# Attention with beacon keys, then a maxout FFN: q and k turned on VectorE in 32x32 blocks, scores in four 32-row tiles

## The chip, the cores and the metric

The kernel runs on one core of a Trainium2 chip. The metric is device time in microseconds of one execution; the time before is the median of 3 runs, 336.58 us (336.32 to 336.59). A core has TensorE (PE; its weight loads are listed apart as PEld), VectorE (DVE), ScalarE (ACT), GpSimd (POOL) and SyncE (SP), each with its own instruction queue that it works through in order, and 16 DMA engines. SBUF is the working memory with 128 partitions; matrix products land in PSUM, which has 8 banks of 512 fp32 values per partition. All 8 banks are taken in both kernels.

## The reference

```python
# q, k, v: (8, 8, 576, 64) fp32; beacon_k, beacon_v: (8, 8, 16, 64)
k_all = np.concatenate([beacon_k, k], axis=2)          # 592 keys
v_all = np.concatenate([beacon_v, v], axis=2)
scores = scale * np.matmul(q, k_all.transpose(0, 1, 3, 2))
scores = np.where(causal, -1000000000.0, scores)       # beacons are never masked
scores = scores - scores.max(-1, keepdims=True)
a = np.exp(scores)
a /= a.sum(-1, keepdims=True) + 1e-09
attn = np.matmul(a, v_all)                             # (8, 8, 576, 64)
x = attn.transpose(0, 2, 1, 3).reshape(4608, 512)
h = np.maximum(np.maximum(x @ w1, x @ w2), x @ w3)     # (4608, 768)
out = h @ w_out                                        # (4608, 512) fp32
```

## The kernel before

All products are in bf16 with fp32 sums. For each batch of 576 tokens the eight heads are worked in four pairs ("p", 32 pairs in all), and two pairs make a quad of four heads (16 quads).

**Preparing q and k.** `load_pair` (L155) brings two heads of q and of k to 96 partitions with six tokens on each (token = 6*partition + r). `cast_pair` makes bf16 copies, mostly on POOL (L172). `turn` (L186) transposes them on PE, six 96x128 blocks for q, six for k and one small block for the beacons (L194, L200), into one PSUM bank each; `evac_q` and `evac_k` (L210, L217, L218) copy the result to SBUF on DVE. Queries stay in the order (r, partition), keys go back to token order. Each of the two heads of a pair gets its own 128-partition query tile `qz` whose other 64 partitions are zero, so that a product over 128 rows gives one head's scores.

**Scores.** A pair's 592 keys lie in five key tiles of 128 (the last has 80). `emit_scores` (L291) takes one of six chunks: per head one matmul (L306) into a PSUM bank of `sc_psum` (4 buffers) and one exponential on ACT (L314) into `at_sb`. The causal edge is put to zero on POOL, one `affine_select` per head (L332); in batch 0 a product with a mask on DVE does it (L329).

**Probabilities times values.** `pv_pass` (L344) works four heads at once in four 32-column tiles of the PE array: a pass with ones gives the sums (then Ln and Exp(-x) on ACT, L366 and L368), two passes with the even and odd columns of v give the outputs, which DVE multiplies by the reciprocals into `xT` (L373), a ring of four batches. `emit_pv` runs six such passes per quad, in three steps of two.

**FFN.** Blocks of 512 tokens; a block has 18 units of four matmuls (L396), each evacuated by ACT (the first of three, L404) or by a maximum on DVE (the other two, L406), and four units of six matmuls (L413) whose result DVE copies (L421) and SP stores (L429, two or three stores per tile because of the token order). Both kinds use `ffn_psum`, two buffers. 9 blocks make 198 units.

**Order.** Everything is emitted by hand in `emit_all` (L528): per chunk the scores, at some chunks a PV step of the quad before, the next pair's transposes, then the planned casts and loads (`at_step`, L499 on), filler matmuls in the first batch (`keep_busy`, L229), and FFN units as far as a running allowance and the finished batches let them. FFN units start with the second batch. The tail after the last PV step is FFN alone.

Of the kernel before, what the change touches and what calls it, by code (L numbers as in the profile page):

```python
# [16 lines left out]
def kernel(  # L17
# [27 lines left out]
    QR = 6  # L45
    QP = S // QR

    n_kt = (NK + 127) // 128
    k_rows = [min(128, NK - 128 * t) for t in range(n_kt)]

    k_tok = [128 * t - Nb for t in range(n_kt)]
    p_min = [max(0, t0) // QR for t0 in k_tok]
    p_max = [min(QP, -(-(k_tok[t] + k_rows[t]) // QR)) for t in range(n_kt)]
    q_wide = [QP - p0 for p0 in p_min]
    at_off = [QR * sum(q_wide[:t]) for t in range(n_kt + 1)]
    RH = QR // 2
    HALF = RH * QP
    n_quad = 2
    n_jj = H // (2 * n_quad)
    PPB = H // 2  # L60
    NPAIR = B * PPB

    RING = 4

    def head(g, j):
        return 4 * g + j

    def place(p):
        b, pi = divmod(p, PPB)
        return b, pi // n_jj, 2 * (pi % n_jj)  # L70
# [8 lines left out]
    st_pool = ctx.enter_context(tc.tile_pool(name="st", bufs=10))  # L79
    pair_pool = ctx.enter_context(tc.tile_pool(name="pair", bufs=3))  # L80
    bk_pool = ctx.enter_context(tc.tile_pool(name="bk", bufs=2))
    v_pool = ctx.enter_context(tc.tile_pool(name="v", bufs=2))
    kt_pool = ctx.enter_context(tc.tile_pool(name="kt", bufs=2))
# [4 lines left out]
    sc_psum = ctx.enter_context(tc.tile_pool(name="sc_psum", bufs=4, space=PSUM))  # L88
# [3 lines left out]

    busy = const.tile([128, 320], BF16, name="busy")
    nc.vector.memset(busy, 1.0)
    ident = const.tile([128, 128], BF16)
    make_identity(nc, ident)
    ones = const.tile([128, 32], BF16)
    nc.scalar.preload_act_table_set("natural_log_exp_and_others")


    NQZ = 2
    qz = []
    for i in range(NQZ):
        pair = []
        for e in range(2):
            z = const.tile([128, QR, QP], BF16, name=f"qz{i}{e}")
            nc.vector.memset(z[64 * (1 - e) : 64 * (1 - e) + 64], 0.0)
            pair.append(z)
        qz.append(pair)
    nc.vector.memset(ones, 1.0)  # L110


    MW = max(p_max[t] - p_min[t] for t in range(n_kt))
    mask = const.tile([128, n_kt, QR, MW], BF16, name="mask")
    nc.gpsimd.memset(mask, 1.0)
    for t in range(n_kt):
        nc.gpsimd.affine_select(
            out=mask[:, t],
            in_=mask[:, t],
            compare_op=ALU.is_ge,  # L120
            fill=0.0,
            base=QR * p_min[t] - k_tok[t],
            pattern=[[1, QR], [QR, MW]],
            channel_multiplier=-1,
        )


    STW = 4 * QR * D
    stage = {}

    def new_stage(key):
        stage[key] = st_pool.tile([128, STW], FP32, name="st")
        return stage[key]

    tiles = {}

    def v_tile(b):
        if b not in tiles:
            tiles[b] = v_pool.tile([128, n_kt, H, D], BF16, name="v_sb")
        return tiles[b]  # L140

    NQ2 = 2 * QR * D

    def load_beacon_k(b):
        st = bk_pool.tile([Nb, H, D], FP32, name="bk32")
        stage["bk", b] = st
        nc.sync.dma_start(out=st, in_=beacon_k[b].rearrange("h n d -> n h d"))

    def cast_beacon_k(b, cast):
        st = stage.pop(("bk", b))  # L150
        bk16 = bk_pool.tile([Nb, H, D], BF16, name="bk16")
        stage["bk16", b] = bk16
        cast(bk16, st)

    def load_pair(p, k_queue=None):  # L155
        b, g, j0 = place(p)
        hs = slice(head(g, j0), head(g, j0) + 2)
        st = new_stage(("pair", p))
        if g == 0 and j0 == 0:
            load_beacon_k(b)  # L160
        for i, (src, queue) in enumerate(((q, nc.sync), (k, k_queue or nc.sync))):
            queue.dma_start(
                out=st[0:QP, i * NQ2 : (i + 1) * NQ2].rearrange("p (h x) -> p h x", h=2),
                in_=src[b, hs].rearrange("h (p r) d -> p h (r d)", r=QR),
            )

    def cast_piece(p, i, cast, r0=0, r1=QR):

        st = stage["pair", p]
        if ("pair16", p, i) not in stage:  # L170
            stage["pair16", p, i] = pair_pool.tile([QP, QR, 2, D], BF16, name=f"p16{i}")
        cast(  # L172
            stage["pair16", p, i][:, r0:r1].rearrange("p r h d -> p h r d"),
            st[0:QP, i * NQ2 : (i + 1) * NQ2].rearrange(
                "p (h r d) -> p h r d", h=2, r=QR
            )[:, :, r0:r1],
        )

    def cast_pair(p, q_cast, k_cast):
        cast_piece(p, 0, q_cast)  # L180
        cast_piece(p, 1, k_cast)
        stage.pop(("pair", p))

    turned = {}

    def turn(p, i):  # L186
        b, g, j0 = place(p)
        src = stage.pop(("pair16", p, i))
        pool, name = (ffn_psum, "fps") if b == 0 else (sc_psum, "sc")
        ps = pool.tile([128, NK], BF16, name=name)  # L190
        if i == 1:
            bk16 = stage["bk16", b]
            h0 = head(g, j0)
            nc.tensor.transpose(  # L194
                ps[:, 0:Nb],
                bk16[:, h0 : h0 + 2].rearrange("p h d -> p (h d)"),
                ident[0:Nb, 0:Nb],
            )
        for r in range(QR):
            nc.tensor.transpose(  # L200
                ps[:, Nb + r * QP : Nb + (r + 1) * QP],
                src[:, r].rearrange("p h d -> p (h d)"),
                ident[0:QP, 0:QP],
            )
        return ps

    def evac_q(p, ps, copy=None):
        for e in range(2):
            hs = slice(64 * e, 64 * e + 64)
            (copy or nc.vector.tensor_copy)(  # L210
                qz[p % NQZ][e][hs], ps[hs, Nb:NK].rearrange("d (r p) -> d r p", r=QR)
            )

    def evac_k(p, ps):
        kT = kt_pool.tile([128, NK], BF16, name="kT")
        turned[p] = kT
        nc.vector.tensor_copy(kT[:, 0:Nb], ps[:, 0:Nb])  # L217
        nc.vector.tensor_copy(  # L218
            kT[:, Nb:NK].rearrange("d (p r) -> d p r", r=QR),
            ps[:, Nb:NK].rearrange("d (r p) -> d p r", r=QR),  # L220
        )

    def emit_transposes(p):
        q_ps = turn(p, 0)
        k_ps = turn(p, 1)
        evac_q(p, q_ps)
        evac_k(p, k_ps)

    def keep_busy(n, cols=320):  # L229
        ps = ffn_psum.tile([128, 512], FP32, name="fps")  # L230
        for _ in range(n):
            nc.tensor.matmul(
                ps[:, 0:cols], busy[:, 0:128], busy[:, 0:cols], start=True, stop=True
            )


    T_PIECES = [range(0, 3), range(3, n_kt)]

# [52 lines left out]
    def emit_scores(p, c, between=None):  # L291
# [28 lines left out]
        if between is not None:  # L320
            between()
# [281 lines left out]
```

## Time and profile before

| | before |
|---|---|
| median of 3 runs | 336.58 us |
| span of the profiled execution | 335.0 us (its own time outside the span is not listed apart; the median is 1.6 us more) |
| mean granted TensorE clock | 0.991 |
| PE busy | 317.1 us, 95% |
| DVE, ACT, POOL busy | 188.5, 186.7, 178.3 us |
| scores on PE (L306) | 384 matmuls, 77.5 us |
| exponentials (L314) | 384, 131.2 us |
| causal edge on POOL (L332) | 336, 93.5 us |
| moved by DMA | 42.02 MB, mean 125 GB/s |

The span runs from the first to the last instruction. Matmuls are pipelined: the time that one costs the PE is the distance to the next start, not the length of its own row, which holds its latency too. A row "x6" of the timeline merges six instructions that follow each other.

### The profile page before, as it was taken

What the parts mean: (1) busy time and instruction counts of PE and PEld (TensorE: products, weight loads), DVE (VectorE), ACT (ScalarE), POOL (GpSimd) and SP (SyncE); (2) the same over time, 40 slices, a digit from 0 to 9 for tenths busy, and PEclk for the clock granted to TensorE, in tenths of its full rate; (3) what the DMA queues carried; (4) which work ended last, traced back from release to release, by engine and by line L of the source; (5) the groups of instructions that cost most, each with busy time, mean ns of one, the idle gap of its engine ahead of it and who ended that gap; (6) DMA issues with size and microseconds to landing.
All of it is one profiled execution on the core that took longest, in us unless ns stands there. A gap on an engine that the chain in (4) does not pass through costs nothing.

```text
span 335.0 us, 9369 instructions
## 1 busy us (share of the span) xinstructions
PE 317.1 (95%) x3703; PEld 184.6 (55%) x3703; DVE 188.5 (56%) x368; ACT 186.7 (56%) x506; POOL 178.3 (53%) x469
## 2 busy tenths in 40 slices
PE   5886899996999999999999999999999999999994
PEld 2554556553555556555555878655555555544441
DVE  3675556662566556565666556555656465555553
ACT  3676667654766476747675667657664765220220
POOL 4778496646674686549564956485847733000000
PEclk9799999999999999999999999999999999999998
DMA  7999999998942681549162847130003001302204
GB/s 189 228 258 247 194 224 237 224 233 207 269 103 62 184 230 43 106 114 258 51 143 66 253 98 146 41 89 4 2 23 104 3 2 31 97 2 59 67 2 125
DMA packets 62971, 42.02 MB, mean 125 GB/s; under 512 B 42192, under 2 KB 58320, under 8 KB 62928
## 3 DMA queue, kind: packets, MB, share of 16 engines
q1 hardware_dynamic: 58672, 37.99, 47.7%
q0 software_dynamic: 4048, 3.15, 5.9%
q8 instruction: 29, 0.48, 0.6%
q10 hardware_dynamic: 208, 0.29, 0.3%
q14 instruction: 14, 0.11, 0.1%
HBM read 35.13 MB, written 9.44 MB: 133 GB/s over the span
## 4 chain that ended last, share of the span: by engine, by line
PE 86%; DVE 4%; ACT 4%; DMA 2%; SPq 1%; issue 1%; POOL 1%; DVEq 0%; ACTq 0%; POOLq 0%
PE fps L396 37%; PE sc L306 12%; PE fps L413 12%; PE pv L354 12%; PE sc L200 5%; PE sc L396 5%; ACT at_sb L314 3%; PE sc L413 2%; DVE at_sb L329 2%; DMA st<-in_q_dram 1%; PE sc L194 1%; DMA out_dram<-y 1%; DVE qz L210 1%; PE fps L200 1%; SPq L251 1%
## 5 line engine op out<-in xcount | busy, mean ns | idle before, releaser
L314 ACT ACTIVATE at_sb<-sc 128x288 bf16<-128x288 f32 (+4 forms) x384 | 131.2, 403 | 65.1 <-PE sc L306 57.5
L396 PE MATMUL fps<-xT,w_sb 128*128 128x512 bf16 (+1 forms) x648 | 147.1, 356 | 2.7 <-DVE y L421 2.2
L332 POOL TENSOR_SCALAR_AFFINE_SELECT at_sb<-at_sb 128x57 bf16<-128x57 bf16 (+1 forms) x336 | 93.5, 297 | 93.1 <-ACT at_sb L314 88.6
L396 PEld LDWEIGHTS <-w_sb 128*128 128x128 bf16 x720 | 66.8, 98 | 52.8 <-issue 3.2
L406 DVE TENSOR_TENSOR hT<-hT,fps 128x512 bf16<-128x512 bf16 x96 | 65.9, 686 | 52.2 <-PE fps L396 39.6
L306 PE MATMUL sc<-qz,kT 128*128 128x288 bf16 (+4 forms) x384 | 77.5, 286 | 5.9 <-ACT at_sb L314 3.9
L306 PEld LDWEIGHTS <-kT 128*128 128x128 bf16 (+1 forms) x384 | 38.0, 101 | 39.4 <-issue 5.2
L172 POOL CAST p<-st 96x768 bf16<-96x768 f32 x60 | 48.3, 829 | 7.6 <-DMA st<-in_k_dram 6.6
L404 ACT CAST hT<-fps 128x512 bf16<-128x512 f32 x48 | 28.1, 585 | 40.7 <-PE fps L396 40.4
L373 DVE TENSOR_TENSOR xT<-pv,recip 128x288 bf16<-128x288 f32 x64 | 27.7, 454 | 34.9 <-ACT recip L368 30.1
L413 PE MATMUL fps<-w_out_sb,hT 128*128 128x512 bf16 x192 | 46.8, 380 | 0.0
L421 DVE COPY y<-fps 128x512 f32<-128x512 f32 x32 | 22.1, 690 | 22.4 <-PE fps L413 12.2
L354 PE MATMUL pv<-at_sb,v_sb 128*32 128x288 bf16 (+4 forms) x1280 | 32.4, 237 | 0.0
L354 PEld LDWEIGHTS <-v_sb 128*32 128x32 bf16 (+1 forms) x1280 | 25.5, 96 | 11.8 <-issue 10.8
L413 PEld LDWEIGHTS <-hT 128*128 128x128 bf16 x216 | 19.5, 98 | 20.2 <-DVE hT L406 0.4
L210 DVE COPY qz<-sc 64x576 bf16<-64x576 bf16 x56 | 25.3, 451 | 8.1 <-PE sc L200 7.7
L200 PE MATMUL sc<-ident,p 96*128 96x96 bf16 x336 | 23.9, 207 | 0.1
L260 POOL CAST v_sb<-st 128x512 bf16<-128x512 f32 (+1 forms) x40 | 23.3, 614 | 0.6 <-DMA st<-in_v_dram 0.5
L200 PEld LDWEIGHTS <-p 96*128 96x128 bf16 x384 | 19.8, 98 | 6.4 <-DVE p L172 2.7
L218 DVE COPY kT<-sc 128x576 bf16<-128x576 bf16 x28 | 20.9, 748 | 0.0
L396 PE MATMUL sc<-xT,w_sb 128*128 128x512 bf16 x72 | 18.5, 379 | 0.0
L354 PE MATMUL pv<-at_sb,ones 80*32 80x42 bf16 (+4 forms) x640 | 17.9, 238 | 0.6 <-DVE xT L373 0.5
(36 smaller groups left out, 135.1 us busy)
## 6 DMA issues: line engine op xcount, KB each, us to landing
st<-in_q_dram SPq DMA_DIRECT2D x32, 288.0 KB, 5.1
st<-in_k_dram SPq DMA_DIRECT2D x31, 288.0 KB, 6.0
st<-in_v_dram SPq DMA_DIRECT2D x24, 256.0 KB, 4.6
out_dram<-y SPq DMA_DIRECT2D x24, 192.0 KB, 2.5
out_dram<-y SPq DMA_DIRECT2D x24, 128.0 KB, 2.4
w_sb<-in_moe_w_dram POOLq DMA_DIRECT2D x12, 192.0 KB, 9.1
st<-in_v_dram SPq DMA_DIRECT2D x8, 224.0 KB, 5.8
out_dram<-y SPq DMA_DIRECT2D x24, 64.0 KB, 2.0
```

The lines of the kernel that those rows point to most:

```text
L172: cast(stage["pair16", p, i][:, r0:r1].rearrange("p r h d -> p h r d"), st[0:QP, i * NQ2 : (i + 1) * NQ2].rearrange("p (h r d) -> p h r d" ...
L200: nc.tensor.transpose(ps[:, Nb + r * QP : Nb + (r + 1) * QP], src[:, r].rearrange("p h d -> p (h d)"), ident[0:QP, 0:QP],)
L210: (copy or nc.vector.tensor_copy)(qz[p % NQZ][e][hs], ps[hs, Nb:NK].rearrange("d (r p) -> d r p", r=QR))
L306: nc.tensor.matmul(ps[0:n, 0 : nr * w].rearrange("k (r p) -> k r p", p=w), kT[:, 128 * t : 128 * t + n], qz[p % NQZ][e][:, r0:r1, p0:QP], ...
L314: nc.scalar.activation(out=at_view(at_sb, t, j0 + e, r0, r1), in_=sc[e][0:n, 0 : nr * w], func=AF.Exp, scale=scale,)
L332: nc.gpsimd.affine_select(out=view[:, e], in_=view[:, e], compare_op=ALU.is_ge, fill=0.0, base=QR * p0 + r0 - k_tok[t], pattern=[[1, nr], ...
L354: nc.tensor.matmul(ps[32 * j : 32 * j + 32, :, p_min[t] : QP], lhsT, at_view(at_sb, t, j, hf * RH, (hf + 1) * RH).rearrange("k (r p) -> k ...
L373: nc.vector.tensor_mul(xs.rearrange("c (r p) -> c r p", p=QP), ps, recips[hf])
L396: nc.tensor.matmul(ps[:, o0 : o0 + n], w_in[i][:, ct, 128 * ft : 128 * (ft + 1)], xT[:, ct, x0 : x0 + n], start=(ct == 0), stop=(ct == n_c ...
L404: nc.scalar.copy(hT[:, ft, :], ps)
L406: nc.vector.tensor_max(hT[:, ft, :], hT[:, ft, :], ps)
L413: nc.tensor.matmul(ps, hT[:, ft, 128 * tt : 128 * (tt + 1)], w_out_sb[:, ft, :], start=(ft == 0), stop=(ft == n_ft - 1),)
```

## The change

q and k are loaded four heads at a time, 32 partitions per head and 18 tokens on each (token = 18*partition + s). After the cast to bf16 one DVE instruction transposes 36 blocks of 32x32, so that head h has its dimensions on partitions 32h to 32h+31, in two halves j of 32 dimensions side by side, and the tokens in order. A score block is then a sum over the two halves, of products over 32 rows, and the four heads go to four row tiles of the PE array and to four PSUM banks. Key tiles are put together in four bursts per quad. One exponential takes two banks, one `affine_select` four heads. The PE transposes, their evacuations, the zeroed query tiles, the mask tile and the filler matmuls are gone. Tokens are in order everywhere, so one store writes an output tile. A step is now a burst of a quad (16 x 4 steps): PV passes of the quad before, scores, planned work, FFN units.

```diff
-    QR = 6
-    QP = S // QR
+    HG = 4
+    n_quad = H // HG
+    NQ = B * n_quad
+    QS = S // 32
+    DJ = D // 32
+    q_min = [max(0, 128 * t - Nb) for t in range(n_kt)]
+    NKP = 128 * n_kt
+    bursts = [
+        [(0, 0, HALF), (3, q_min[3], S)],
+        [(0, HALF, S), (4, q_min[4], S)],
+        [(1, q_min[1], S)],
+        [(2, q_min[2], S)],
+    ]
...
-    sc_psum = ctx.enter_context(tc.tile_pool(name="sc_psum", bufs=4, space=PSUM))
+    sc_psum = ctx.enter_context(tc.tile_pool(name="sc_psum", bufs=2, space=PSUM))
...
+    def load_qk(Q, which, queue=None):
+        b, g = divmod(Q, n_quad)
+        st = st_pool.tile([128, QS * D], FP32, name="st")
+        src = (q, k)[which][b, HG * g : HG * (g + 1)]
+        (queue or nc.sync).dma_start(
+            out=st, in_=src.rearrange("h (p s) d -> (h p) (s d)", s=QS)
+        )
...
+    def turn(Q, which, s0=0, s1=QS):
+        src = stage[Q, which, 16][:, s0 * D : s1 * D]
+        dst = qTs[Q % 2] if which == 0 else kTs[Q % 2][:, :, Nb:NK]
+        nc.vector.transpose(
+            dst.rearrange("p j (t s) -> p s j t", s=QS)[:, s0:s1],
+            src.rearrange("p (s j d) -> p s j d", j=DJ, d=32),
+        )
+
+    def turn_beacon(Q):
+        nc.vector.transpose(
+            kTs[Q % 2][:, :, 0:Nb], bk16[:, Q].rearrange("p (j n) -> p j n", j=DJ)
+        )
...
+    def emit_scores(Q, c):
+        sc = [sc_psum.tile([128, 2, 512], FP32, name="sc") for _ in range(HG // 2)]
+        off = 0
+        for t, q0, q1 in bursts[c]:
+            w = q1 - q0
+            for j in range(DJ):
+                for h in range(HG):
+                    hs = slice(32 * h, 32 * h + 32)
+                    nc.tensor.matmul(
+                        sc[h // 2][:, h % 2, off : off + w],
+                        kT[hs, j, 128 * t : 128 * (t + 1)],
+                        qT[hs, j, q0:q1],
+                        start=(j == 0),
+                        stop=(j == DJ - 1),
+                        tile_position=(32 * h, 0),
+                    )
+            off += w
+        a0, a1 = burst_at[c]
+        for i in range(HG // 2):
+            nc.scalar.activation(
+                out=at_sb[:, 2 * i : 2 * i + 2, a0:a1], in_=sc[i][:, :, 0:off],
+                func=AF.Exp, scale=scale,
+            )
...
+                nc.gpsimd.affine_select(
+                    out=view, in_=view, compare_op=ALU.is_ge, fill=0.0,
+                    base=q0 - (128 * t - Nb),
+                    pattern=[[0, HG], [1, edge - q0]],
+                    channel_multiplier=-1,
+                )
...
-    PV_ORDER = [(0, 0), (0, 1), (0, 2), (1, 0), (1, 1), (1, 2)]
+    PV_ORDER = [(0, 0), (1, 0), (0, 1), (0, 2), (1, 1), (1, 2)]
...
+        nc.sync.dma_start(out[c0 : c0 + 128, :], y)
...
+    at_step(0, 0, L(cast_qk, 1, 1, by_pool), L(turn, 1, 1), L(turn_beacon, 1))
+    at_step(0, 1, L(cast_qk, 1, 0, by_pool), L(turn, 1, 0))
+    at_step(0, 2, *[L(load_w, i, 0, FH) for i in range(3)])
+    at_step(0, 3, L(load_qk, 2, 1, nc.scalar), L(load_qk, 2, 0, nc.scalar))
+    at_step(1, 0, L(cast_v, 0, 0, 2, by_pool), L(cast_beacon_k, 1, B, by_pool))
+    at_step(1, 1, L(cast_v, 0, 2, 4, by_pool))
+    at_step(1, 2, L(cast_v, 0, 4, 5, by_pool))
...
+    for Q in range(2, NQ):
+        b, g = divmod(Q, n_quad)
+        at_step(Q - 1, 1, L(cast_qk, Q, 1, by_pool))
+        at_step(Q - 1, 2, L(turn, Q, 1), L(turn_beacon, Q), L(cast_qk, Q, 0, by_pool))
+        at_step(Q - 1, 3, L(turn, Q, 0))
...
+        first = 3 * NC
+        rate = (len(units) - 2 * 22 - 6) / (NQ * NC - first)
+        for Q in range(NQ):
+            b, g = divmod(Q, n_quad)
+            for c in range(NC):
+                if Q > 0 and c > 0:
+                    emit_pv(Q - 1, c - 1)
+                emit_scores(Q, c)
+                for fn in plan.pop((Q, c), ()):
+                    fn()
+                if c == 3 and g == 0 and b > 0:
+                    ready = b - 1
+                if Q * NC + c >= first - 1:
+                    allowed += rate
+                while emit_ffn(allowed, ready):
+                    pass
```

469 lines of the change are left out of this document (145 added, 324 removed).

## The prediction

> **What bounds the kernel now.** I read the page first: the engines' shares, the clock and the chain that ended last.
>
> ```profile
> span 335.0 us, 9369 instructions
> PE 317.1 (95%) x3703; PEld 184.6 (55%) x3703; DVE 188.5 (56%) x368; ACT 186.7 (56%) x506; POOL 178.3 (53%) x469
> PEclk9799999999999999999999999999999999999998
> PE 86%; DVE 4%; ACT 4%; DMA 2%; SPq 1%; issue 1%; POOL 1%; DVEq 0%; ACTq 0%; POOLq 0%
> ```
>
> TensorE is the bound, at full clock but for the second slice. Its own distances come from the chain in order of time (first and last pieces of a batch, and the last of all) and from the timeline of PE; a window of that batch gives the engines' busy time in it.
>
> ```profile
> 114.85 0.86 PE fps L396 x4
> 150.04 0.86 PE fps L396 x4
> 329.06 1.31 PE fps L413 x6
> ```
>
> ```profile
> 114.80:150.00 35.20, 35.20 (x439) 20.19 (x436) 20.80 (x40) 22.67 (x62) 22.51 (x62) 1.00 0.53 133
> ```
>
> ```profile
> 41.00 1.03 PE L396 MATMUL fps<-xT,w_sb 128*128 128x512 bf16 x4
> 154.22 0.45 PE L306 MATMUL sc<-qz,kT 128*128 128x336 bf16 x2
> 154.50 0.42 PE L200 MATMUL sc<-ident,p 96*128 96x96 bf16 x6
> 154.86 0.18 PE L194 MATMUL sc<-ident,bk 16*128 16x16 bf16 x1
> 154.97 0.43 PE L200 MATMUL sc<-ident,p 96*128 96x96 bf16 x6
> 155.23 1.03 PE L396 MATMUL fps<-xT,w_sb 128*128 128x512 bf16 x4
> 158.33 0.41 PE L306 MATMUL sc<-qz,kT 128*128 128x288 bf16 x2
> 158.67 0.56 PE L354 MATMUL pv<-at_sb,ones 128*32 128x288 bf16 x20
> 159.06 0.54 PE L354 MATMUL pv<-at_sb,v_sb 128*32 128x288 bf16 x20
> 159.52 1.04 PE L396 MATMUL fps<-xT,w_sb 128*128 128x512 bf16 x4
> ```
>
> From start to start: an FFN unit takes 0.86 us (six matmuls 1.30), two score matmuls of 336 columns 0.28 (154.22 to 154.50), so 0.417 ns a column. A pair's transposes take 0.73 (154.50 to 155.23). Six of them alone take 0.26 (154.97 to 155.23) but 0.36 where a 16-row one follows: changing the array's row tiling costs 0.10 each way. A PV pass of 837 columns for four heads takes 0.39, the second 0.46 with the way back; two matmuls of 288 columns (0.24) stand 0.34 ahead of the first, another 0.10. A PV step so costs 0.95. A batch repeats every 35.19 us (114.85 to 150.04) and PE (the first busy time of the window's row, 35.20) has no idle in it.
>
> Sum for before: FFN starts at 41.0; 162 x 0.86 + 36 x 1.30 = 186; PV of 14 quads 14 x 3 x 0.95 = 39.9; scores of the 27 pairs still to come, 3348 columns each, 27 x 1.40 = 37.8; 26 pairs' transposes 19.0; from the last matmul's end (330.4) to the end 4.6. That is 328.3 of 335.0, so 6.7 us of waits. The median is 1.6 us over this span; I add that at the end.
>
> **The change on PE.** Transposes: minus 19.0. PV: nearly the same columns (1664 for 1674), 32 instructions for 40: 0.94 a step, 39.5. Scores: a quad has 1664 query columns times two halves. If the four row tiles run together, that is 3328 x 0.417 = 1.39 us for four heads, where two pairs took 2.79; if one after another, 5.55. The nearest row is the PV pass, four column tiles of 837 columns in 0.39 where one alone would stream 0.35: I take together, plus 0.1 for 48 instructions and five more changes of tiling (in and out at the first burst, out at three) at 0.10: 2.0 a quad, 26 for the 13 quads after FFN starts.
>
> By the Trainium skill, "TensorE: Matmul & The Clock Gate", section "Measured speedup vs the span model", four row tiles gave 3.07 times, not four; 5.55/3.07 = 1.81 a quad adds 5.5 us as an estimate. No row here has a row tile beside another.
>
> **The other engines.** These groups by line and shape carry their prices.
>
> ```profile
> L314 ACT ACTIVATE at_sb<-sc 128x468 bf16<-128x468 f32 x64 | 32.4, 558 | 12.9 <-PE sc L306 12.2
> L314 ACT ACTIVATE at_sb<-sc 128x210 bf16<-128x210 f32 x64 | 18.8, 347 | 23.1 <-PE sc L306 20.2 <-DVE at_sb L329 2.9
> L366 ACT ACTIVATE lnd<-pv 128x288 f32<-128x288 f32 x32 | 13.6, 424 | 6.5 <-PE pv L354 5.8
> L368 ACT ACTIVATE recip<-lnd 128x288 f32<-128x288 f32 x32 | 14.2, 443 | 1.0
> L404 ACT CAST hT<-fps 128x512 bf16<-128x512 f32 x48 | 28.1, 585 | 40.7 <-PE fps L396 40.4
> L406 DVE TENSOR_TENSOR hT<-hT,fps 128x512 bf16<-128x512 bf16 x96 | 65.9, 686 | 52.2 <-PE fps L396 39.6 <-PE sc L306 11.2
> L373 DVE TENSOR_TENSOR xT<-pv,recip 128x288 bf16<-128x288 f32 x64 | 27.7, 454 | 34.9 <-ACT recip L368 30.1 <-PE pv L354 4.9
> L218 DVE COPY kT<-sc 128x576 bf16<-128x576 bf16 x28 | 20.9, 748 | 0.0
> L210 DVE COPY qz<-sc 64x576 bf16<-64x576 bf16 x56 | 25.3, 451 | 8.1 <-PE sc L200 7.7
> L217 DVE COPY kT<-sc 128x16 bf16<-128x16 bf16 x28 | 4.7, 166 | 0.9
> L332 POOL TENSOR_SCALAR_AFFINE_SELECT at_sb<-at_sb 128x132 bf16<-128x132 bf16 x168 | 52.9, 328 | 67.9 <-ACT at_sb L314 65.1
> L332 POOL TENSOR_SCALAR_AFFINE_SELECT at_sb<-at_sb 128x57 bf16<-128x57 bf16 x112 | 27.6, 257 | 20.7 <-ACT at_sb L314 18.9
> L172 POOL CAST p<-st 96x768 bf16<-96x768 f32 x60 | 48.3, 829 | 7.6 <-DMA st<-in_k_dram 6.6
> L260 POOL CAST v_sb<-st 128x512 bf16<-128x512 f32 x32 | 18.8, 613 | 0.5 <-DMA st<-in_v_dram 0.5
> L270 POOL DMA_DIRECT2D w_sb<-in_moe_w_dram x12 | 8.7, 724 | 0.0
> ```
>
> Exponentials: (558-347)/258 = 0.82 ns an element and 0.175 fixed, so a burst's two take 1.97, 1.55, 1.87 and 1.45 us, 6.84 a quad (before 131.2/16 = 8.2 by the table). Edges: 0.95 ns and 0.20 fixed, 0.51 to 0.69 each, 3.2 a quad (before 93.5/16 = 5.8). Casts of 1152 elements: 0.84 ns more each beyond the 829 row, 1.15; of 1024, 1.04. All three lose work.
>
> A turn of 1152 elements has no row. Slope of the strided copy over its short form, (748-166)/560 = 1.04 ns: 1.35 us. At the rate of L210, (451-166)/560, it would be 0.75; at two strided passes 2.5. I take 1.35, as it too moves every element to a strided place. A quad then costs DVE 2 x 1.35 + 0.17, where the four evacuations of two pairs cost 3.6. The Trainium skill, "VectorE: DVE Perf Modes", section "The three transpose paths", gives 311 ns for a 128x128 bf16 turn on VectorE; nine of these would be 2.8 us.
>
> DMA and SP: the same bytes in larger pieces, one store per output tile: nothing on the path, since the loads run a quad or more ahead; without that lead a quad's 1.18 MB would cost 4.7 us at the 250 GB/s below.
>
> **The start.** The timeline's first rows, and the rate in 0.75 us slices of the first 30 us:
>
> ```profile
> 4.73 0.51 ACT L172 CAST p<-st 96x384 bf16<-96x384 f32 x1 [2.64 <-DMA st<-in_k_dram]
> 8.34 0.65 PE L306 MATMUL sc<-qz,kT 128*128 128x288 bf16 x2 [0.93 <-DVE kT L218]
> 8.79 0.71 ACT L314 ACTIVATE at_sb<-sc 128x288 bf16<-128x288 f32 x2 [0.51 <-PE sc L306]
> ```
>
> ```profile
> GB/s 0 0 48 241 278 242 256 252 248 250 248 250 254 246 255 226 224 203 217 218 218 218 209 246 221 211 270 283 289 263 267 279 273 280 273 300 328 266 248 262
> ```
>
> Now k and q of four heads, 1.18 MB, come first: at 250 GB/s from 2.2 us they are there at 6.9. Half a cast (576 elements) on ACT 0.67, turn of k 1.35, beacons 0.17, turn of q 1.35, handovers 0.3: scores at 10.7 instead of 8.34. FFN may start after 11 more steps. Paced by ACT that would be 10.7 + 2.75 x 6.84 + 2 quads of Ln and Exp (2 x 1.73) + 12 gaps of 0.45 (8.34 to 8.79) = 38. But score banks are no longer doubled (a burst fills all four), so each gap is on the path, and with the filler matmuls gone I expect half clock here, some 0.4 more a gap: 43. And POOL stands ahead: six weight issues (4.4 us) are queued before the edge of quad 0's last burst, which the first PV pass needs; PE waits for it with the scores behind. The v casts stand behind the edges of quad 1, so the second and third PV steps wait as well. Carried through: quad 0's exponentials end at 13.7, 16.2, 19.2 and 21.5, the weight issues at 24.3, the edge behind them at 25.0, where PV starts. Quad 1's exponentials end at 24.6, 29.3 and 34.9; behind their edges (and POOL's 0.55 for the beacons) the v casts end at 27.4, 30.9 and 36.2, and each PV step starts there. Quad 2's scores start at 40.6, and three bursts with two Ln and Exp pairs and four gaps take it to FFN at 50 us instead of 41.0; ends 38 and 56.
>
> **New waits in the steady steps.** A step now is PV 0.95, scores 0.5, about 2.85 FFN units, near 3.9 us. ACT has (6.84 + 2 x 0.87 + 3 copies of 0.585)/4 = 2.6 of work in it, DVE (4 x 0.454 + 2.87 + 8 x 0.69)/4 = 2.6. But there are two FFN buffers, and each engine works in order. Counted from the scores' start, FFN starts at 0.5; the exponentials run from 0.7 to 2.1 (last burst) to 2.7 (first), and behind Ln and Exp to 3.0 at the second burst. Where the step's first unit is one that ACT evacuates, its copy ends 0.6 later; the third unit, ready at 2.3, needs that buffer: 0.5 to 1.3 us lost. The program's order has 17 such steps: 12.4 us. Where DVE evacuates the first unit, a turn in front of it (0.6 to 2.0, then 0.69) delays the third by 0.5: 6 steps, 3. Three steps have no FFN unit at all, so the next scores wait for the exponentials: 3 x 1.25. Sum 19. What covers these evacuations before is that FFN units stand singly between chunks.
>
> ```profile
> DVE y L421 <- DMA out_dram<-y: 6.3, 2, 5.1
> ```
>
> The chain of waits shows that output copies already wait for stores behind loads; I keep 4 us for it.
>
> Sum: 50 + 186 + 39.5 + 26 + 19 + 4 + end 4.6 + 1 (the last PV step, with FFN waiting on its products) = 330.1; with 1.6 the median is 331.7, say 332: 1.4% faster.
>
> **Rivals.**
> - *Waits hidden.* FFN starts at 42 and a third of the 19 stays: 332 - 8 - 13 = 311. For it: PE shows no idle in a batch though DVE and ACT are half busy. Against: exponentials are now in lumps of 1.5 to 2 us.
> - *Slower: the turn holds DVE.* At 2.5 us each, FFN evacuations queue behind it: 1.15 more on about ten steps, 2.3 more at the start and 0.7 in quad 1: 332 + 14.5 = 346. It decides from 1.7 us a turn on (the margin of 4.9 us over 13 turns is 0.37). For it: no row bounds a block turn; against: DVE copies here cost about 1 ns an element. The Trainium skill's 311 ns, above, speaks for it.
> - *Weight loads of the four tiles in turn.* Six transposes with their loads take 0.26, so a load costs at most 0.043; four in turn make every pass at least 0.17, a quad 2 x (5 x 0.17 + 0.19) = 2.1 instead of 1.39, and 13 quads 9 us: 341, slower; it decides from 0.38 a quad. PV's loads, of 32 columns, show no such cost; no row excludes it for 128. The Trainium skill's 3.07 would make it 337, no change.
> - *Row tiles one after another:* 13 x (5.55 - 1.39) = 54, so 386. PV's 20 matmuls in 0.39 speak against it; the place would be the scores' line.
>
> **How the numbers follow.** Forecast 0.40 (321 to 336), waits hidden 0.17, turn 0.28, loads in turn 0.08, serial tiles 0.07. About 0.2% is what a measurement here can tell from no change; the same gets 0.03 of the loads' 0.08 and 0.01 from the forecast's upper edge, and 0.01 of the loads' share falls on the faster side: faster 0.40 + 0.17 - 0.01 + 0.01 = 0.57, same 0.04, slower 0.28 + 0.04 + 0.07 = 0.39. The range 308 to 350 leaves out serial tiles and some 0.06 at the ends.
>
> **What would show it.** In the changed profile: four score matmuls starting within some 10 ns of each other and a quad near 2.0 us; a turn at 1.35 us; first FFN matmul near 50 us; PE idle of some 0.4 us a step, put down to ACT copies or DVE maxima. Wrong it would be by a turn over 1.7 us, by tiles that queue, by a clock that stays down after FFN starts, or by evacuations that wait in more than the 26 steps counted.

## The result, and the profile after

The changed kernel takes 441.67 us (median of 4 runs, 440.75 to 444.43) where the kernel before takes 336.58 us (336.32 to 338.07): 1.314 times as long, with an interval of 1.308 to 1.319. The forecast was 332.0 with a range of 308 to 350, so it was wrong in sign and far outside the range. Three rivals had the sign: the turn holds DVE (346), weight loads in turn (341) and row tiles one after another (386). Only the first of them names the engine that the profile shows below.

The page of the changed kernel: engines, granted clock, and the chain that ended last.

```profile
span 439.1 us, 7604 instructions
PE 308.1 (70%) x3199; PEld 145.6 (33%) x3240; DVE 282.2 (64%) x260; ACT 159.3 (36%) x249; POOL 110.3 (25%) x154
PEclk9999995968989898879798897889789897999999
PE 46%; DVE 28%; issue 13%; ACT 6%; POOL 4%; DMA 1%; DVEq 0%; POOLq 0%
PE fps L299 23%; DVE qT L146 15%; PE fps L316 9%; PE pv L264 5%; PE sc L210 5%; ACT at_sb L221 5%; DVE kT L146 5%; PE sc L299 3%; DVE hT L309 3%; DVE xT L280 3%; POOL w_sb L187 1%; PE sc L316 1%; DMA st<-in_k_dram 1%; POOL at_sb L233 1%; DVE kT L154 1%
```

PE was busy for 95% of the span before and 86% of the chain was its own; now 70% and 46%. The chain has 20% in the two turns (L146, `kT` and `qT`), and the clock row has slices at five to eight tenths throughout the middle. The groups by line give the reason:

```profile
L146 DVE STREAM_TRANSPOSE kT<-c 128x1152 bf16<-128x1152 bf16 x16 | 82.3, 5144 | 8.8 <-POOL c L136 8.5
L146 DVE STREAM_TRANSPOSE qT<-c 128x1152 bf16<-128x1152 bf16 x16 | 81.6, 5099 | 0.3 <-POOL c L136 0.3
L221 ACT ACTIVATE at_sb<-sc 128x992 bf16<-128x992 f32 (+3 forms) x128 | 103.3, 859 | 135.8 <-PE sc L210 135.8
L233 POOL TENSOR_SCALAR_AFFINE_SELECT at_sb<-at_sb 128x512 bf16<-128x512 bf16 (+2 forms) x80 | 46.7, 593 | 266.8 <-ACT at_sb L221 265.1
```

One turn takes 5.1 us, not 1.35. The 32 turns hold DVE for 164 us, where the evacuations that they replace (L210, L217, L218) took 57. ACT and POOL did lose work, as forecast: 159.3 for 186.7 us and 110.3 for 178.3.

The view of waits over all engines, over the whole span (us in total, times, longest):

```profile
DVE hT L309 <- PE fps L299: 72.8, 44, 2.9
PE fps L299 <- DVE hT L309: 52.2, 14, 6.6
PE sc L210 <- DVE qT L146: 44.2, 8, 16.8
```

Three of the eight waits of the scores (16.8, 7.0 and 5.8 us) lie ahead of the first FFN matmul. The same view for PE, from there to the last PV matmul (61.7 to 393.7 us), has

```profile
PE sc L210 <- DVE qT L146: 14.7, 5, 3.8
PE fps L299 <- DVE xT L280: 7.4, 3, 3.8
```

beside the same 52.2. PE waits for DVE, and DVE waits for PE, in turn. The timelines of DVE and of PE for the same 20 us show how:

```profile
107.71 0.81 DVE L280 TENSOR_TENSOR xT<-pv,recip 128x288 bf16<-128x288 f32 x2
108.61 5.12 DVE L146 STREAM_TRANSPOSE kT<-c 128x1152 bf16<-128x1152 bf16 x1
113.38 0.38 DVE L154 STREAM_TRANSPOSE kT<-bk 128x32 bf16<-128x32 bf16 x1
113.52 1.36 DVE L324 COPY y<-fps 128x512 f32<-128x512 f32 x2
117.33 5.10 DVE L146 STREAM_TRANSPOSE qT<-c 128x1152 bf16<-128x1152 bf16 x1
126.67 1.48 DVE L309 TENSOR_TENSOR hT<-hT,fps 128x512 bf16<-128x512 bf16 x2 [2.93 <-PE fps L299]
```

```profile
108.06 2.76 PE L316 MATMUL fps<-w_out_sb,hT 128*128 128x512 bf16 x11
114.34 1.46 PE L316 MATMUL fps<-w_out_sb,hT 128*128 128x512 bf16 x6 [3.52 <-DVE y L324]
122.49 0.74 PE L210 MATMUL sc<-qT,kT 32*128 32x288 bf16 x16 [2.25 <-DVE qT L146]
123.16 4.26 PE L299 MATMUL fps<-xT,w_sb 128*128 128x512 bf16 x12
127.35 0.90 PE L264 MATMUL pv<-at_sb,ones 128*32 128x288 bf16 x32
```

At 108.6 the turn of k goes into DVE's queue ahead of two copies of FFN results. PE fills both FFN buffers and then stands for 3.5 us, until the copies behind the turn give one back. At 117.3 the turn of q follows, and the next quad's scores stand for it. Neither shows as a slow evacuation: the copies take 0.68 us each as before.

The windows from the first FFN matmul to the last PV matmul. The columns are length, then busy time and count of PE, weight loads, DVE, ACT and POOL, then granted clock, DMA share and GB/s:

```profile
61.70:393.70 332.00, 244.36 (x2675) 116.70 (x2712) 225.10 (x208) 128.79 (x204) 82.63 (x112) 0.88 0.28 80
```

These 332 us hold 53 steps. DVE has 225.1/53 = 4.2 us of work in each, PE 244.4/53 = 4.6 (4.0 at full clock, from the dense kernel below). Yet a step takes 332/53 = 6.3: neither engine is full, and (244.4 + 225.1 - 332)/53 = 2.6 us of their work a step is the least that lies side by side; the trace has 2.7. PE is idle for 87.6 us of the 332 and DVE for 106.9.

### The profile page after: what moved, and what is told of

Same layout as the page of the kernel before. It is cut to its first block, busy times and chain, and to the rows that moved or that the text cites. A ratio compares the mean times of both kernels' runs of the same rounds, so it can differ in the third digit from the quotient of the medians.

```text
span 439.1 us, 7604 instructions
## 1 busy us (share of the span) xinstructions
PE 308.1 (70%) x3199; PEld 145.6 (33%) x3240; DVE 282.2 (64%) x260; ACT 159.3 (36%) x249; POOL 110.3 (25%) x154
## 4 chain that ended last, share of the span: by engine, by line
PE 46%; DVE 28%; issue 13%; ACT 6%; POOL 4%; DMA 1%; DVEq 0%; POOLq 0%
PE fps L299 23%; DVE qT L146 15%; PE fps L316 9%; PE pv L264 5%; PE sc L210 5%; ACT at_sb L221 5%; DVE kT L146 5%; PE sc L299 3%; DVE hT L309 3%; DVE xT L280 3%; POOL w_sb L187 1%; PE sc L316 1%; DMA st<-in_k_dram 1%; POOL at_sb L233 1%; DVE kT L154 1%
## 5 line engine op out<-in xcount | busy, mean ns | idle before, releaser
L299 PE MATMUL fps<-xT,w_sb 128*128 128x512 bf16 (+1 forms) x618 | 160.2, 402 | 67.6 <-DVE hT L309 52.2
L221 ACT ACTIVATE at_sb<-sc 128x992 bf16<-128x992 f32 (+3 forms) x128 | 103.3, 859 | 135.8 <-PE sc L210 135.8
L233 POOL TENSOR_SCALAR_AFFINE_SELECT at_sb<-at_sb 128x512 bf16<-128x512 bf16 (+2 forms) x80 | 46.7, 593 | 266.8 <-ACT at_sb L221 265.1
L146 DVE STREAM_TRANSPOSE kT<-c 128x1152 bf16<-128x1152 bf16 x16 | 82.3, 5144 | 8.8 <-POOL c L136 8.5
L146 DVE STREAM_TRANSPOSE qT<-c 128x1152 bf16<-128x1152 bf16 x16 | 81.6, 5099 | 0.3 <-POOL c L136 0.3
L210 PE MATMUL sc<-qT,kT 32*128 32x288 bf16 (+4 forms) x768 | 45.0, 327 | 49.6 <-DVE qT L146 44.2
L210 PEld LDWEIGHTS <-kT 32*128 32x128 bf16 x768 | 17.2, 101 | 70.3 <-DVE qT L146 31.5
L136 POOL CAST c<-st 128x1152 bf16<-128x1152 f32 (+1 forms) x31 | 35.0, 1128 | 0.0
L177 POOL CAST v_sb<-vst 128x1024 bf16<-128x1024 f32 (+1 forms) x24 | 21.5, 895 | 0.0
L264 PE MATMUL pv<-at_sb,ones 128*32 128x288 bf16 (+4 forms) x512 | 15.8, 268 | 0.0
L276 ACT ACTIVATE recip<-lnd 128x288 f32<-128x288 f32 x32 | 14.2, 443 | 1.0
## 6 DMA issues: line engine op xcount, KB each, us to landing
out_dram<-y SPq DMA_DIRECT2D x36, 256.0 KB, 2.0
vst<-in_v_dram SPq DMA_DIRECT2D x24, 256.0 KB, 5.4
```

The lines of the kernel that those rows point to most:

```text
L136: cast(stage[Q, which, 16][:, cols], stage[Q, which][:, cols])
L146: nc.vector.transpose(dst.rearrange("p j (t s) -> p s j t", s=QS)[:, s0:s1], src.rearrange("p (s j d) -> p s j d", j=DJ, d=32),)
L210: nc.tensor.matmul(sc[h // 2][:, h % 2, off : off + w], kT[hs, j, 128 * t : 128 * (t + 1)], qT[hs, j, q0:q1], start=(j == 0), stop=(j == D ...
L221: nc.scalar.activation(out=at_sb[:, 2 * i : 2 * i + 2, a0:a1], in_=sc[i][:, :, 0:off], func=AF.Exp, scale=scale,)
L233: nc.gpsimd.affine_select(out=view, in_=view, compare_op=ALU.is_ge, fill=0.0, base=q0 - (128 * t - Nb), pattern=[[0, HG], [1, edge - q0]], ...
L264: nc.tensor.matmul(ps[32 * j : 32 * j + 32, lo - h0 : hi - h0], lhsT, at_sb[0:n, j, a : a + hi - lo], start=(i == 0), stop=(i == len(runs) ...
```

## The experiments

The theory after this profile: the turn is slow because of where it writes. Its blocks are spread so that neighbouring elements of one block land 18 tokens, 36 bytes, apart; the time that this holds DVE explains the whole loss. Rivals: a block turn is slow whatever it writes; the layout makes PE's reads slow too; or it is the place of casts and turns in the queues, not their length. Each kernel is read against the kernel before on the same chip: 337.17 us for the dense, copied, paired and reloaded kernels, 339.12 for the turn four times over, in pieces, the price table and e8_spread, and 336.58 (median of 7) for e8_timed, e9_start and e12_rate.

### Dense writes: e1_dense

The same turns, but each block is written to 32 neighbouring columns.

```diff
-            dst.rearrange("p j (t s) -> p s j t", s=QS)[:, s0:s1],
+            dst.rearrange("p j (s t) -> p s j t", s=QS)[:, s0:s1],
```

> One edit to the changed kernel: a turn writes its 32-token runs side by side instead of 18 tokens (36 bytes) apart. Queries and keys then stand in another order than the causal edge and v assume, so the output is not the reference's; the work on every engine is the same. Theory S (the strided write makes the turn slow): the turn falls from 5.1 us to about 1.35 and the kernel to about 332, the forecast's own sum. Theory B (a turn of 36 blocks of 32x32 costs 5.1 us however it writes): turn 5.1, kernel 441.

Measured: 323.07 us. The groups and the windows of this kernel:

```profile
L146 DVE STREAM_TRANSPOSE kT<-c 128x1152 bf16<-128x1152 bf16 x16 | 21.9, 1371 | 8.8 <-POOL c L136 8.4
L146 DVE STREAM_TRANSPOSE qT<-c 128x1152 bf16<-128x1152 bf16 x16 | 22.0, 1373 | 5.4 <-POOL c L136 5.2
```

```profile
48.70:275.90 227.20, 213.68 (x2675) 108.20 (x2712) 131.26 (x206) 127.75 (x204) 82.40 (x112) 1.00 0.43 124
```

One stride changed and the turn went from 5.12 to 1.37 us, as theory S had it, and the span from 439.1 to 321.3; the kernel's time lies 9 us below the 332 expected. The 117.8 us between them come apart by these windows: 13.0 in the start (first FFN matmul at 61.7 and 48.7), 87.6 - 13.5 = 74.1 of PE idle between FFN start and last PV, and 244.4 - 213.7 = 30.7 in which PE was busy longer for the same 2675 matmuls, at a granted clock of 0.88 for 1.00. The tails are the same (45.4).

### A copy to the same places: e2_copy

The turn is replaced by a copy with the same strided target; the transposition is left out.

```diff
-        nc.vector.transpose(
+        nc.vector.tensor_copy(
```

> One edit to the changed kernel: a plain DVE copy with the same source and the same strided destination stands in place of each turn of q and k; the transposition is left out, so the output is not the reference's. Theory S: the copy takes about 5 us as well and the kernel about 440. Theory B: the copy takes about 1.35 us (1152 elements at 1.04 ns and 0.17) and the kernel about 332.

Measured: 367.23 us.

```profile
L146 DVE COPY qT<-c 128x1152 bf16<-128x1152 bf16 x16 | 47.7, 2984 | 5.1 <-POOL c L136 5.1
L146 DVE COPY kT<-c 128x1152 bf16<-128x1152 bf16 x16 | 43.9, 2746 | 8.8 <-POOL c L136 8.4
L233 POOL TENSOR_SCALAR_AFFINE_SELECT at_sb<-at_sb 128x512 bf16<-128x512 bf16 (+2 forms) x80 | 84.0, 1060 | 153.0 <-ACT at_sb L221 152.8
```

A plain copy to these places takes 2.7 to 3.0 us, which neither theory had (5 and 1.35). So the places alone cost, and a turn pays nearly twice as much for them. The mean edge went from 593 to 1060 ns, though its own data did not change. The median stayed at 634 and the longest took 3140: in the trace the 30 edges that overlap a copy take 1.88 us in the mean, the other 50 take 0.57. POOL slowed as well as DVE.

### Pairs of elements: e3_pairs

Two neighbouring bf16 values are moved as one 4-byte element. A block then turns 32 tokens by 32 pairs, writes are 72 bytes apart, and the two halves of a head are the even and odd dimensions. PE reads every second element of both operands.

```diff
+        src = stage[Q, which, 16][:, s0 * D : s1 * D].bitcast(FP32)
+        dst = dst.rearrange("p n e -> p (n e)").bitcast(FP32)
         nc.vector.transpose(
-            dst.rearrange("p j (t s) -> p s j t", s=QS)[:, s0:s1],
-            src.rearrange("p (s j d) -> p s j d", j=DJ, d=32),
+            dst.rearrange("p (t s) -> p s t", s=QS)[:, s0:s1],
+            src.rearrange("p (s i) -> p s i", i=32),
...
-                        kT[hs, j, 128 * t : 128 * (t + 1)],
-                        qT[hs, j, q0:q1],
+                        kT[hs, 128 * t : 128 * (t + 1), j],
+                        qT[hs, q0:q1, j],
```

> The turn moves pairs of bf16 as one 4-byte element: 576 elements, 18 blocks instead of 36, written 72 bytes apart; a head's even and odd dimensions take the place of its two halves, and the matmuls read every second element. Theory S, a cost per write: turn about 576 x 4.4 ns = 2.5 us, kernel about 346 by the price that the slower rival gave. Theory B: a cost per block gives 2.5 us too, a cost per byte 5.1 us and 441. PE reads of every second element are expected to cost nothing; score passes over 0.45 ns a column would show that they do.

Measured: 321.92 us.

```profile
L147 DVE STREAM_TRANSPOSE kT<-c 128x576 f32<-128x576 f32 x16 | 20.1, 1257 | 9.8 <-POOL c L136 8.3
L147 DVE STREAM_TRANSPOSE qT<-c 128x576 f32<-128x576 f32 x16 | 20.0, 1250 | 5.0 <-POOL c L136 5.0
```

Half as many writes, twice as far apart, take a quarter of the time, half of what a fixed cost per write or per block gave (2.5 us, 346 us), and tokens stay in order. PE's strided reads cost little: from FFN start to the last PV the scores take 26.4 us of PE here and 25.6 in the dense kernel (summed from start to start).

### Order bought by the loads: e5_smajor

Dense writes, with tokens in order because each load brings token 32*s + partition, in pieces of 256 bytes and four transfers per load.

```diff
-            out=st, in_=src.rearrange("h (p s) d -> (h p) (s d)", s=QS)
+                out=st[32 * h : 32 * h + 32].rearrange("p (s d) -> p s d", d=D),
+                in_=src[h].rearrange("(s p) d -> p s d", p=32),
```

> The loads put token 32*s + partition on each partition, in pieces of 256 bytes (four DMAs a load), so that a turn's runs of 32 tokens lie side by side and in token order. Theory S: turn about 1.35 us, kernel about 332, plus up to 5 us if the smaller pieces make the start's loads late. Theory B: turn 5.1 us, kernel about 441.

Measured: 344.93 us, with turns of 1.37 us. The first scores came at 14.2 us and FFN at 66.0, for 10.2 and 48.7 in the dense kernel, so 17.3 of the 21.9 us that it takes over the dense kernel lie in the start, more than the 5 expected. The first loads, which have no lead, cost 4.0 of them. The largest piece is a wait of 12.5 us of the scores for ACT's exponentials, and the timeline of ACT shows what holds them:

```profile
24.73 15.48 ACTq L129 DMA_DIRECT2D st<-in_q_dram  x4
40.26 1.89 ACT L223 ACTIVATE at_sb<-sc 128x992 bf16<-128x992 f32 x2 [16.46 <-DMA vst<-in_v_dram]
```

Quad 2's q is loaded from ACT's queue, now by four transfers. Issuing them takes 15.5 us, and quad 1's exponentials stand behind them in that queue; the view puts the wait down to a load of v, which ended last. Whether the same pieces issued from SP's queue would cost less was not tried.

### Time alone: e6_dense_x4

The dense turn, issued four times over: DVE is held as long as by the strided turn, with no strided write anywhere.

```diff
+        for _ in range(4):
             nc.vector.transpose(
                 dst.rearrange("p j (s t) -> p s j t", s=QS)[:, s0:s1],
```

> The turn with side-by-side writes (1.37 us) is issued four times over, so that DVE is held for 5.5 us a turn without one strided write; order of queries and keys as in the run with side-by-side writes, so not the reference's output. Theory T1 (all of the loss is DVE time in front of the FFN evacuations and of the scores): 441 to 455. Theory T2 (strided writes also slow the other engines' reads and writes of SBUF): clearly under 441, by as much as that costs.

Measured: 456.26 us. Its waits:

```profile
PE sc L211 <- DVE qT L147: 56.1, 10, 17.9
PE fps L300 <- DVE hT L310: 46.8, 12, 7.7
```

4 x 1.375 = 5.5 us a turn gives the same two waits, 102.9 us together where 5.1 us gave 96.4. The time is 1 us above the upper end of theory T1. So no side effect of the strided write is needed: DVE's time explains the loss. The granted clock fell here too, to 0.86 between FFN start and last PV.

### The turn in pieces: e7_pieces

From quad 2 on the strided turn is cut into three parts of 1.87 us, two of them put behind later FFN units, so that no evacuation stands behind 5 us.

```diff
+    def in_pieces(Q, which):
+        turn(Q, which, 0, 6)
+        later.append(L(turn, Q, which, 6, 12))
+        later.append(L(turn, Q, which, 12, QS))
```

> The changed kernel with each turn from quad 2 on cut into three instructions of six tokens (strided as before, about 1.7 us each), the second and third placed behind one FFN unit each. DVE does the same work. Theory H (FFN evacuations held behind one long instruction, two FFN banks run out): the steady part loses at most 1.7 us at a time and the kernel falls to about 390. Theory Q (the quad is paced by the row cast, turn of k, turn of q, scores): no gain, 435 or more.

Measured: 429.31 us.

```profile
PE sc L210 <- DVE qT L146: 58.0, 11, 16.7
PE fps L299 <- DVE hT L309: 31.0, 20, 5.0
```

Neither theory's figure came (390, or 435 and more). FFN waits less (52.2 to 31.0) and the scores wait more (44.2 to 58.0): two parts in three of a turn now stand behind FFN units, so it ends later. Cutting the hold and moving its parts is worth 12 of 105 us in sum; the two effects are not told apart here. Nor was a place further ahead tried, a whole quad before the scores that need the turn.

### The price of a place: e10_strides

Twenty-eight instructions on DVE behind the work of the kernel with pairs: turns and copies of the same data whose target distance alone changes.

```diff
+            op(
+                dst.rearrange("p (a t g) -> p a g t", t=32, g=g),
+                src.rearrange("p (a g t) -> p a g t", t=32, g=g),
+            )
```

> The kernel with turns by pairs, and behind its end on DVE 28 single instructions over 1152 bf16 or 576 fp32 values, turn and plain copy, with the destination's elements 1, 2, 3, 4, 6, 9, 18 and 36 (fp32: 1, 2, 3, 6, 9, 18) places apart and the source dense. Only these instructions' times matter; the kernel's own time grows by their sum, 50 to 90 us. Theory S with a threshold in bytes: flat at about 1.37 us for the bf16 turn up to some distance, then a step to 5.1, and the copy to 2.5 to 3.0, at the same number of bytes for both types. Theory S without one: growing with the distance all along.

The line's own view gives the extremes (shortest, median, longest in ns):

```profile
L444 DVE STREAM_TRANSPOSE c<-c x14: 779/1412/5212, 318.3 to 350.8; 128x1152 bf16<-128x1152 bf16 x8, 128x576 f32<-128x576 f32 x6
L444 DVE COPY c<-c x14: 459/962/2703, 352.1 to 371.3; 128x1152 bf16<-128x1152 bf16 x8, 128x576 f32<-128x576 f32 x6
```

Each from the trace, in ns, by the distance of neighbouring writes in elements:

| | 1 | 2 | 3 | 4 | 6 | 9 | 18 | 36 |
|---|---|---|---|---|---|---|---|---|
| turn, 1152 bf16 | 1378 | 1447 | 2082 | 2724 | 4001 | 5208 | 5098 | 5212 |
| turn, 576 fp32 | 779 | 779 | 942 | - | 1193 | 1202 | 1259 | - |
| copy, 1152 bf16 | 460 | 804 | 1121 | 2703 | 2081 | 2689 | 2628 | 2682 |
| copy, 576 fp32 | 459 | 754 | 553 | - | 1169 | 679 | 707 | - |

Neither form of the theory came out whole: there is no single step. The bf16 turn grows with the distance, by some 640 ns per element from 2 to 6, and is flat at 5.1 to 5.2 us from 9 elements (18 bytes) on: 4.5 ns a write. The 4-byte turn rises to 1.26, 2.2 ns a write. A bf16 copy to far places costs half as much as a turn. The copy at 4 and the fp32 copies at 2 and 6 stand out of line; each is one instruction, and I leave them open.

The Trainium skill, "SBUF — State Buffer", section "Door 1: The DMA port swizzle (why `[64,N]` ≈ `[32,N]`)", says that memory is organised in lines of 16 bytes, that an access which crosses to a new line pays, and that 8 bf16 or 4 fp32 of distance are therefore free. The flat part from 18 bytes on agrees. "Free" does not: at 4 bf16, two writes to a line, the turn already took 2724 ns for 1378. The measurement decides.

### The forecast's timetable: e12_rate and e8

Two changes to the order of the kernel with pairs: the allowance of FFN units per step from 148/52 = 2.846 to 22/8 = 2.75 (e12_rate), and besides it one unit emitted ahead of a step's scores (e8).

```diff
-        rate = (len(units) - 2 * 22 - 6) / (NQ * NC - first)
+        rate = 22 / (2 * NC)
...
+                emit_ffn(allowed + rate, ready)
                 emit_scores(Q, c)
```

> The turn by pairs, and two changes of the order: one FFN unit stands between the PV passes and the scores, ahead of the exponentials in ACT's queue, and the FFN allowance is 22 units per 8 steps, so that no step is left without one. By the forecast's timetable the 17 steps that lose 0.5 to 1.3 us (12.4) and the three without a unit (3.75) should go: about 16 off 322, so 306 to 312. If those waits were not what PE idles for, it stays at 320 or more.

> As e3 (turns in pairs) with the allowance alone changed, from 148/52 = 2.846 units a step to 22/8 = 2.75, so that no step is without a unit; no unit ahead of the scores. The forecast's split of the waits (three unit-less steps 3.75 us, 23 steps with an evacuation behind exponentials or turns 15.4) says: 3 to 4 us less than e3's 321.92, so 318 to 319, the rest of e8's gain coming from the unit ahead of the scores. Rival (the steps without units made all of it): 311 to 313. Rival (the allowance changes nothing): 321 to 322.5.

> The same kernel as e8_spread (turns in pairs, one FFN unit ahead of each step's scores, allowance 2.75 units a step), timed against the kernel before in turns. Theory: the one look was no accident: 310 to 312 us, ratio to before 0.92 to 0.93. Rival (one look caught a chance good run): above 318.

Measured: both changes 310.99 us, then 310.51 (310.33 to 310.55), 0.921 times the kernel before with an interval of 0.916 to 0.927. The allowance alone: 313.33. PE's waits with pairs alone, from FFN start on, and for the allowance alone in the same stretch:

```profile
PE fps L299 <- ACT hT L307: 5.1, 7, 0.8
PE fps L299 <- DVE hT L309: 3.2, 6, 0.9
PE sc L210 <- ACT at_sb L221: 1.1, 3, 0.4
```

```profile
PE fps L299 <- DVE hT L309: 4.0, 6, 0.7
```

My expectation of 318 to 319 for the allowance was wrong, because it took the two kinds of step apart. By the program's order 17 steps before begin with a unit that ACT evacuates and have a third one behind it, and three have no unit; at 2.75 no step is empty, and the seven that begin with such a unit have only two. One number removed both kinds. With the unit ahead of the scores the DVE wait went too: PE was idle for 0.7 us from FFN start to last PV. The waits of this timetable were of the kinds that the forecast named; it had priced 19 us, and they measured 13.5 (dense) and 12.5 (pairs). By kind, in the kernel with pairs: behind ACT's copy 5.1 us in 7 waits (12.4 in 17 steps forecast), behind DVE's maximum 3.2 in 6 (3 in 6), scores behind exponentials 1.1 in 3 (3.75 in 3).

### The start: e9_start

On top of e8: the casts of quad 1 and of batch 0's v on DVE instead of POOL, and the weight issues a step later.

```diff
-    at_step(0, 0, L(cast_qk, 1, 1, by_pool), L(turn_beacon, 1), L(turn, 1, 1))
+    at_step(0, 0, L(cast_qk, 1, 1, by_dve), L(turn_beacon, 1), L(turn, 1, 1))
...
-    at_step(0, 2, *[L(load_w, i, 0, FH) for i in range(3)])
+    at_step(0, 3, *[L(load_w, i, 0, FH) for i in range(3)])
...
-    at_step(1, 0, L(cast_v, 0, 0, 2, by_pool), L(cast_beacon_k, 1, B, by_pool))
+    at_step(1, 0, L(cast_v, 0, 0, 2, by_dve), L(cast_beacon_k, 1, B, by_pool))
```

> As e8, and at the start alone: the casts of quad 1's k and q and of batch 0's v on VectorE instead of GpSimd, and the six weight issues one step later, behind the edge of quad 0's last burst. The prediction's account of the start (PV waits on GpSimd: weight issues ahead of an edge, v casts behind the edges of quad 1) says: first PV pass whole at 21 to 22 us without the 2.25 us wait for the edge, no wait on v in quad 1, first FFN matmul at 42 to 44 us instead of 47.2, time 305 to 308 us. Rival (ScalarE's exponentials pace the start and GpSimd stands beside them): first FFN matmul at 46 to 47.5 us and time 309.5 to 311.5.

Measured: 306.47 us (306.32 to 307.50), 0.910 times the kernel before, interval 0.904 to 0.917; the fastest of all. The first PV passes of quad 0, in the timeline of PE of e8 and of e9:

```profile
23.70 1.19 PE L264 MATMUL pv<-at_sb,ones 128*32 128x48 bf16 x24 [2.25 <-POOL at_sb L233]
28.75 0.66 PE L264 MATMUL pv<-at_sb,v_sb 128*32 128x48 bf16 x16 [2.38 <-POOL v_sb L177]
46.54 1.10 PE L299 MATMUL fps<-xT,w_sb 128*128 128x512 bf16 x3
```

```profile
20.94 1.58 PE L264 MATMUL pv<-at_sb,ones 128*32 128x288 bf16 x32
23.55 0.91 PE L264 MATMUL pv<-at_sb,v_sb 128*32 128x288 bf16 x24
41.82 0.60 PE L299 MATMUL fps<-xT,w_sb 128*128 128x512 bf16 x2
```

The waits on POOL's edge and v casts are gone and FFN starts 4.7 us earlier, at 41.8. So POOL's queue did gate the start, as the prediction had it. The casts and the weight issues were moved in one run, so their shares are not known.

## Why the prediction was wrong

**The step that failed is the turn's price** ("The other engines"): 1.35 us was taken, with ends of 0.75 and 2.5; it is 5.1. I had taken the slope of the copy at L218 because "it too moves every element to a strided place". It doesn't: the line reads its source 96 elements apart and writes neighbouring places. No DVE row of the profile before wrote single 2-byte elements to separate places, and the upper end (two strided passes) was built from the same wrong kind. A bound from rows has to say on which side the stride lies. That the price is the whole of it is shown by the kernels with dense writes (323.07) and with pairs (321.92): with the turn at 1.37 and 1.25 us the forecast kernel exists, and it lies 9 to 10 us below the 332. A turn over 1.7 us stood on the prediction's own list of signs that it is wrong. The Trainium skill, "VectorE: DVE Perf Modes", section "The three transpose paths", had led to an estimate of 2.8; the dense turn takes half of it and the strided one nearly twice.

**The rival that named the turn was mis-sized twice.** "The turn holds DVE" charged 14.5 us for 1.15 us more a turn. Scaled to 5.12 that would be 14.5 x 3.77/1.15 = 48, so 380. The other 62 us come from its count: it let about ten steps and the start feel the turn. Four kernels that differ in the instructions at the turn's place alone show what a longer hold costs:

| | dense turn | copy | strided turn | four dense turns |
|---|---|---|---|---|
| DVE busy, us | 167.1 | 210.5 | 282.2 | 296.3 |
| span, us | 321.3 | 365.5 | 439.1 | 454.6 |

Against the dense kernel DVE has 43.4, 115.1 and 129.2 us more to do, and the span is 44.2, 117.8 and 133.3 us longer. So over this range the loss is close to all of the added DVE time, 30 to 32 us for each microsecond that every one of the 32 turns grows, where the rival's price was 14.5/1.15 = 12.6. (In the copied kernel POOL's edges were slower as well.) Why it comes out so near one for one is not derived here. For the strided turn the loss has three parts, the 13.0 us of the start, the 74.1 of PE idle and 30.7 from the clock. That PE's idle time lowered the clock was not tried by itself, but the two go together: 0.88 here and 0.86 with the turn four times over, and 1.00 from FFN start to the last PV in the dense, paired and spread kernels, where PE waits at most 0.9 us at a time. In the changed kernel it waits up to 6.6 there. In the timeline of the changed kernel's PE above, the scores at 122.49 waited 2.25 us. The window behind that reads

```profile
122.80:126.30 3.50, 3.50 (x20) 1.23 (x13) 0.84 (x2) 2.36 (x3) 0.97 (x2) 0.51 0.54 219
```

so PE was busy all the time at half clock, and twelve FFN matmuls took from 123.16 to 127.35, 4.19 us, where three units of 0.86 take 2.58. The Trainium skill, "TensorE: Matmul & The Clock Gate", section "Part 1: The HAM clock gate (the "warmup" mystery)", says that the array falls to half rate after an idle window of about 3.4 us. The trace agrees in kind, but the length of one stand does not decide here: the clock fell behind this one of 2.25 us, and behind the 3.52 us before 114.34 it did not (granted clock 1.00 from 114.3 to 118, six matmuls in 1.46 us).

**What held**, measured where the turn no longer covers it:
- *Row tiles run together.* The same burst (two passes of 288 columns and two of 208, merged in one row) of the changed kernel's first quad and of a later one, in the timeline of PE:

```profile
16.79 1.02 PE L210 MATMUL sc<-qT,kT 32*128 32x288 bf16 x16 [16.79 <-DVE qT L146]
...
321.43 0.60 PE L210 MATMUL sc<-qT,kT 32*128 32x288 bf16 x16
321.97 1.90 PE L299 MATMUL fps<-xT,w_sb 128*128 128x512 bf16 x8
```

  Later on, the four passes of four tiles take 0.54 us with the change of tiling. One tile's 992 columns at 0.417 ns make 0.41; tiles one after another would take 1.65, and passes of at least 0.17 for loads in turn 0.68, both before the change of tiling. The 13 quads' scores take 25.6 us of PE in the dense kernel, where 26 was forecast. Serial tiles and loads in turn are refuted.
- *PE's work.* FFN, PV and scores after FFN start take 256.0 us in the dense kernel (195.3, 35.1 and 25.6, summed from start to start, a change of tiling counted to the matmul ahead of it), where 251.5 was forecast (186, 39.5 and 26): FFN 9.3 more and PV 4.4 less, so the sum is nearer than its terms.
- *Exponentials, edges, casts.* A burst's exponentials average 859 ns (forecast 6.84/8 = 855) and the edges take 473 to 637 where 510 to 690 was forecast.
- *The start.* First scores forecast at 10.7: 10.2 dense, 16.8 in the changed kernel. FFN forecast at 50: 48.7 dense, 61.7 changed. The half clock expected there fits the rows above: the same burst takes 1.02 us at first and 0.60 later, although the clock row reads full at both.
- *Waits* of 19 us, and 1 at the last PV step: 12.3 in the dense kernel, in gaps over 0.06 us. The 4 us kept for stores did not come: its waits list no copy that waits for a store. With the start (-1.3), PE's work (+4.5), waits (-7.7), stores (-4) and the end (4.2 for 4.6, from where a next matmul could have started), 330.1 becomes 321.2; the dense span is 321.3.
- *Waits hidden* (311): the changed kernel is not that rival, but the spread kernel, with turns in pairs and another order, comes to its time, 310.5, by another split: FFN starts at 46.5 instead of 42, and 0.7 us of the waits stays instead of a third of 19.

## What to carry to other kernels

Before a DVE instruction is priced by another, compare the distances on both sides of it, and in bytes: here a 2-byte write of a turn to places 18 or more bytes apart cost 4.5 ns, three to four times a dense one, and moving pairs as 4-byte elements brought the turn from 5.1 to 1.25 us without a change of order. When work moves to an engine that also frees the bound engine's buffers, do not take its idle time as room: with DVE busy for little more than half of the dense kernel, each microsecond of work added to it still lengthened the kernel by about as much. Count the order of emission too: one allowance of 2.75 instead of 2.846 units was worth 8.6 us (single runs on two chips, on which the kernel before differs by 0.6).

## What the runs showed that was not expected

- A strided bf16 turn costs twice a strided bf16 copy (5.1 and 2.7 us) and stops growing with the distance at 9 elements; in pairs 72 bytes apart it takes 1.25.
- DVE copies of 2.7 to 3.0 us slowed POOL's edges from 593 to 1060 ns in the mean, while turns of 5.1 us left them at 593.
- A lost quarter of PE's time came back as a lower clock on the rest: 0.88 over 332 us, worth 30.7 us beside 74.1 of added idle.
- Score operands read at every second element cost PE at most 0.8 us in 26.
